# Stage a of an rfft on float16 parts of x, with x read once for its maximum and once more for the products, and its loads on GpSimd's queue

## The chip, the cores and the metric

The kernel runs on one core of one Trainium2 chip. The metric is the device time of one execution in microseconds (us). Before the change the median of 3 runs is 2065.36 us (2063.82 to 2065.78). A separate execution was taken with the hardware profiler; all rows of the trace come from that one.

## The reference

x has 8 batches of 3072 rows by 256 columns, float32. The sequence axis goes through a real FFT, the 256 columns through a complex product with bias and a soft threshold, then the inverse FFT; what comes out is put, row by row, through three products of 256 by 768, their maximum, and a product of 768 by 256.

```
X = np.fft.rfft(x, axis=1)
Yr = Xr @ w_r - Xi @ w_i + b_r
Yi = Xr @ w_i + Xi @ w_r + b_i
Yr = np.sign(Yr) * np.maximum(np.abs(Yr) - lam, 0.0)   # Yi likewise, lam = 0.01
y = np.fft.irfft(Yr + 1j * Yi, n=3072, axis=1)
h = np.maximum(np.maximum(y @ w1, y @ w2), y @ w3)
out = (h @ w_out).astype(np.float32)
```

## The kernel before, in words

**Stages.** The transform of 3072 points is cut into 96 by 32. Stage a is the transform over 96 points (product with the 96x96 table fr): a batch of x is seen as (n1 = 96, n2 = 32, 256 columns) and worked on in eight *quads* of four n2 each; q = 8 * batch + i numbers the quads. A quad has two halves of 96x512. Its result goes through DRAM (a_d). Stage b is the transform over 32 points (tiles px, 12 steps k in a batch), stage w the complex product and the soft threshold (tiles py), stage q a first part of the inverse (tiles pz), whose result goes through DRAM again (z_d). `inverse` (tiles pi) then makes the input yh, yl of the dense part. `up` makes three tiles pu of 128x384 with 18 matmuls of 384 columns, the maximum of which (tiles c and h, lines 757 to 760 on ScalarE and VectorE) is split into float16 halves hh; `down` (tiles pd) multiplies these by w_out with 9 matmuls of 256 columns.

**Products in parts.** A product in high precision is three matmuls (`mm3`, lines 132 to 134): high by high, high by low, low by high. The parts are made by two instructions for a tile: ScalarE writes the high part (line 121 in `split`, 126 in `split_scaled`), VectorE the rest (122, 127). `split_scaled` multiplies by a power of two first. Nearly all parts are float16. Those of stage a are float32r (`x_tile(...).bitcast(F32R)`, fh and fl), and these are made only from quad NATIVE = 16 on, so for batches 2 to 7; batches 0 and 1 take x as it is in one float32 matmul for a half (line 434).

**Stage a in detail.** `load_x` (398) loads a quad, 384 KB, into a tile xq of a pool with two buffers (six quads of batch 0 go to other tiles, xr), by SyncE's queue. `split_x` (410) takes the largest |x| of each half on VectorE (416, tile mxx) and makes the parts. `stage_a` (427) has the matmuls into a PSUM tile pa, ScalarE's copy to SBUF (437) and the store to a_d, by ScalarE's queue (by GpSimd's for batch 0). Behind the last quad of a batch, lines 441 to 452 make the scales of the batch from its largest |x| by a chain of small instructions: s0x scales what `split_a` (459) splits for stage b, s0v the later parts.

**Order.** The dense part goes in *slots*: one slot is one f of `up` and `down`, six for a quad of z, so SLOTS = 48 for a batch, 384 in all. The stages of the next batches are laid between the slots by a list `events` (lines 682 to 702): each entry has a position in slots, a function and its number, and the entries up to a slot's position are run behind that slot. For a quad of batches 2 to 7 the load is at p - 3, `split_x` at p, `stage_a` at p + 1, with p = (b - 2) * 48 + 6i + 2; so a batch's quads are spread over the 48 slots two batches ahead of it, and its stage b to q over the next 48. Batch 1's quads stand at p = i. A scheduler then fixes the order on each engine, and each engine runs its list in order.

## Time and profile before

| | before |
|---|---|
| median of 3 runs | 2065.36 us |
| the profiled execution | 2070.11 us |
| its span, first to last instruction | 2068.3 us |
| granted TensorE clock, mean | 0.995 |
| moved by DMA | 165.13 MB, 80 GB/s in the mean |
| loads of x (xq and xr) | 64 of 384 KB, all by SyncE's queue |

How to read it. PE is TensorE's matmuls, PEld its weight loads, DVE VectorE, ACT ScalarE, POOL GpSimd, SP SyncE; an engine's name with a q behind it is its DMA queue. A group of instructions is told by its line, engine and operation, the tile written, an arrow and the tiles read, the shape, how many there are, then their busy time, the mean of one in ns, and the idle time ahead of them with what ended it. Matmuls overlap, so the mean of one is longer than the distance between two; a timeline, which has each instruction's start, gives the distance. L132 to L134 are the three matmuls of `mm3`, wherever it is called.

### The profile page before, as it was taken

Reading aid. Unit: us, or ns where it says so; the run is one execution under the profiler, and the core shown is the slowest. Engines: PE = TensorE matmul, PEld = TensorE weight load, DVE = VectorE, ACT = ScalarE, POOL = GpSimd, SP = SyncE. Lnnn points to the kernel's source line nnn. Section 1 sums busy time; section 2 is a strip of 40 time slices with the busy share of each in tenths; the row PEclk is TensorE's granted clock in tenths of the full one; section 3 lists DMA queues with packets and bytes.
Section 4 is the critical chain, followed back from the end, with each engine's and each line's share of the span. In section 5 each row is a group of like instructions: output and inputs, shape, how many; then the busy total and the mean of one; then the engine's idle time right before and its main releaser. Section 6 shows DMA issues by size and latency. Waiting matters only on the chain.

```text
span 2068.3 us, 38435 instructions
## 1 busy us (share of the span) xinstructions
PE 2040.7 (99%) x15500; PEld 1431.4 (69%) x15500; DVE 1547.9 (75%) x3043; ACT 1035.0 (50%) x2051; POOL 27.6 (1%) x79
## 2 busy tenths in 40 slices
PE   8999999999999999999999999999999999999998
PEld 5756766677776767767776777767777777776666
DVE  3987897678867888678886788767887578865543
ACT  4755554455545555455554455445554445433333
POOL 1000000000000000000000000000000000000000
PEclk9999999999999999999999999999999999999999
DMA  9454221322213222223213222132221212111100
GB/s 311 141 155 123 90 70 52 107 68 89 75 52 100 79 84 62 65 83 92 85 60 97 62 78 87 47 100 72 86 74 44 77 52 67 42 47 32 34 30 23
DMA packets 106694, 165.13 MB, mean 80 GB/s; under 512 B 9795, under 2 KB 85059, under 8 KB 106419
## 3 DMA queue, kind: packets, MB, share of 16 engines
q1 hardware_dynamic: 45347, 86.69, 14.4%
q10 hardware_dynamic: 60032, 72.37, 10.6%
q0 software_dynamic: 1136, 3.61, 0.5%
q8 instruction: 121, 1.98, 0.4%
q14 instruction: 58, 0.48, 0.1%
HBM read 87.14 MB, written 75.50 MB: 79 GB/s over the span
## 4 chain that ended last, share of the span: by engine, by line
PE 82%; DVE 10%; DMA 3%; ACT 2%; issue 2%; ACTq 0%; SPq 0%; DVEq 0%
PE pu L134 16%; PE pu L132 16%; PE pu L133 16%; PE pd L134 5%; PE pd L132 5%; PE pd L133 5%; PE py L132 2%; PE py L133 2%; PE py L134 2%; DMA xq<-in_x_dram 2%; DVE u L620 1%; PE pi L132 1%; PE pa L434 1%; DVE h L760 1%; PE pa L133 1%
## 5 line engine op out<-in xcount | busy, mean ns | idle before, releaser
L132 PE MATMUL pu<-yh,wuh 128*128 128x384 f16 x2304 | 752.6, 327 | 2.2 <-DVE c L758 1.1
L133 PE MATMUL pu<-yl,wuh 128*128 128x384 f16 x2304 | 751.7, 326 | 0.0
L134 PE MATMUL pu<-yh,wul 128*128 128x384 f16 x2304 | 751.7, 326 | 0.0
L126 ACT ACTIVATE hh<-h 128x384 f16<-128x384 f32 x384 | 200.4, 522 | 512.3 <-DVE h L760 509.8
L134 PEld LDWEIGHTS <-wul 128*128 128x128 f16 x2304 | 225.5, 98 | 148.9 <-issue 1.1
L132 PEld LDWEIGHTS <-wuh 128*128 128x128 f16 x2304 | 225.9, 98 | 143.4 <-issue 14.7
L133 PEld LDWEIGHTS <-wuh 128*128 128x128 f16 x2304 | 225.9, 98 | 135.1 <-issue 5.8
L758 DVE TENSOR_TENSOR c<-pu,c 128x384 f32<-128x384 f32 x384 | 212.5, 554 | 136.8 <-PE pu L134 76.3
L127 DVE SCALAR_TENSOR_TENSOR hh<-h,hh 128x384 f16<-128x384 f32 x384 | 213.6, 556 | 135.3 <-ACT hh L126 132.0
L134 PE MATMUL pd<-woh,hh 128*128 128x256 f16 x1152 | 313.6, 273 | 0.9 <-DVE hh L127 0.8
L132 PE MATMUL pd<-woh,hh 128*128 128x256 f16 x1152 | 313.9, 273 | 0.4 <-ACT hh L126 0.3
L133 PE MATMUL pd<-wol,hh 128*128 128x256 f16 x1152 | 313.8, 273 | 0.0
L760 DVE TENSOR_TENSOR h<-pu,c 128x384 f32<-128x384 f32 x384 | 212.7, 554 | 45.6 <-PE pu L134 33.8
L757 ACT ACTIVATE c<-pu 128x384 f32<-128x384 f32 x384 | 186.0, 484 | 102.7 <-PE pu L134 98.6
L620 DVE SCALAR_TENSOR_TENSOR u<-py,s1x,cs 64x256 f32<-64x256 f32 x308 | 148.5, 482 | 40.9 <-ACT cs L631 30.9
L132 PE MATMUL py<-wch,tt 128*128 128x256 f16 x504 | 137.4, 273 | 0.4 <-DVE yl L127 0.4
L134 PE MATMUL py<-wch,tt 128*128 128x256 f16 x504 | 137.4, 273 | 0.0
L133 PE MATMUL py<-wcl,tt 128*128 128x256 f16 x504 | 137.4, 273 | 0.0
L132 PEld LDWEIGHTS <-hh 128*128 128x128 f16 x1152 | 112.7, 98 | 34.3 <-ACT hh L126 1.0
L133 PEld LDWEIGHTS <-hh 128*128 128x128 f16 x1152 | 112.7, 98 | 33.4
L783 ACT ACTIVATE o<-pd,s1u 128x256 f32<-128x256 f32 x192 | 83.6, 469 | 90.9 <-PE pd L134 53.3
L134 PEld LDWEIGHTS <-hh 128*128 128x128 f16 x1152 | 112.7, 98 | 15.3 <-DVE hh L127 2.0
(205 smaller groups left out, 2889.6 us busy)
## 6 DMA issues: line engine op xcount, KB each, us to landing
aj<-a_d SPq DMA_DIRECT2D x96, 256.0 KB, 2.8
z_d<-zs ACTq DMA_DIRECT2D x96, 256.0 KB, 2.1
out_dram<-o ACTq DMA_DIRECT2D x192, 128.0 KB, 2.1
zq<-z_d SPq DMA_DIRECT2D x63, 384.0 KB, 3.5
xq<-in_x_dram SPq DMA_DIRECT2D x58, 384.0 KB, 4.0
a_d<-aq ACTq DMA_DIRECT2D x56, 384.0 KB, 3.0
rw<-in_moe_w_dram SPq DMA_DIRECT2D x6, 768.0 KB, 9.4
xr<-in_x_dram SPq DMA_DIRECT2D x6, 384.0 KB, 11.4
```

The source lines that it names most:

```text
L126: nc.scalar.activation(out=hi, in_=src, func=AF.Copy, scale=scale)
L127: nc.vector.scalar_tensor_tensor(out=lo, in0=src, scalar=scale, in1=h, op0=ALU.mult, op1=ALU.subtract)
L132: nc.tensor.matmul(o, lh, rh, start=start, stop=False, **kw)
L133: nc.tensor.matmul(o, lh, rl, start=False, stop=False, **kw)
L134: st["mm"] = nc.tensor.matmul(o, ll, rh, start=False, stop=stop, **kw)
L434: nc.tensor.matmul(pa[0:96], fr, xp, start=True, stop=True)
L620: nc.vector.scalar_tensor_tensor(out=u[64 * c:64 * c + 64, j], in0=pk[r], scalar=inv[r], in1=c1[r], op0=ALU.mult, op1=ALU.add,)
L757: nc.scalar.activation(out=c1, in_=pu[0], func=AF.Copy)
L758: nc.vector.tensor_tensor(out=c1, in0=pu[1], in1=c1, op=ALU.max)
L760: nc.vector.tensor_tensor(out=h32, in0=pu[2], in1=c1, op=ALU.max)
L783: nc.scalar.activation(out=o, in_=pd[t], func=AF.Copy, scale=st[b, "su"][1])
```

## The change

- fh and fl become float16 (times 2^10), and the two parts of x for batches 2 to 7 become float16, made by `split_scaled` with a new scale s2x of the batch. The parts of a half lie side by side in one tile: xh for half 0 and xl for half 1. ScalarE's copy behind the matmuls takes a factor 2^-17.
- s2x needs the largest |x| of the whole batch ahead of the parts. So the maximum leaves `split_x` for a function of its own, `largest_x`, and x of batches 2 to 7 is loaded twice: for the maximum at position m - 3 (maximum at m), and for the products at p - 3. m = (b - 3) * 48 + 6i + 5 for batches 3 to 7, that is one batch ahead of the products, and 8 + 2i for batch 2, whose products move from 6i + 2 to 24.5 + 2.9i.
- The chain that makes the scales is now the function `scale_x`, behind the last maximum of a batch (for batch 1 behind its last quad, as before).
- a comes out of stage a already scaled, so `split_a` of batches 2 to 7 uses `split` in place of `split_scaled`.
- x is loaded by GpSimd's queue but for batch 0.

```diff
-    fh = const.tile([N1, 96], F32R, name="fh")
-    fl = const.tile([N1, 96], F32R, name="fl")
+    fh = const.tile([N1, 96], F16, name="fh")
+    fl = const.tile([N1, 96], F16, name="fl")
...
-            nc.sync.dma_start(out=xq.rearrange("p (n d) -> p n d", n=NQ), in_=xv)
+            eng = nc.sync if q < NCH else nc.gpsimd
+            eng.dma_start(out=xq.rearrange("p (n d) -> p n d", n=NQ), in_=xv)
...
+    def largest_x(q):
+        b, q4 = divmod(q, NCH)
+        for i, xp in enumerate(st["x", q]):
+            nc.vector.tensor_reduce(
+                out=batch(b, "x")[0:N1, 2 * q4 + i:2 * q4 + i + 1], in_=xp, axis=AX.X,
+                op=ALU.max, apply_absolute_value=True,
+            )
+        if b > 1 and q4 == NCH - 1:
+            scale_x(b)
+    def scale_x(b):
+        low, add = st["lim", "x"]
+        e = exponent_of(st.pop((b, "x"))[0:N1], "x", 23, 0xFF, low)
+        st[b, "sx"] = power("s0x", e, -1.0, 261.0), power("s1x", e, 1.0, add)
+        if b > 1:
+            st[b, "sx2"] = power("s2x", e, -1.0, 268.0)
...
             if q >= NATIVE:
-                xh, xl = (x_tile(n).bitcast(F32R)[0:N1] for n in ("xh", "xl"))
-                split(xh, xl, xp)
+                t = x_tile(("xh", "xl")[i]).bitcast(F16)[0:N1]
+                xh, xl = t[:, 0:2 * D], t[:, 2 * D:4 * D]
+                split_scaled(xh, xl, xp, st[b, "sx2"][0:N1])
...
-            nc.scalar.activation(out=aq[:, i * 512:i * 512 + 512], in_=pa[0:96], func=AF.Copy)
+            nc.scalar.activation(
+                out=aq[:, i * 512:i * 512 + 512], in_=pa[0:96], func=AF.Copy,
+                scale=1.0 if q < NATIVE else A_SCALE,
+            )
...
-        split_scaled(ah, al, aj, st[k // NJP, "sx"][0])
+        if k // NJP > 1:
+            split(ah, al, aj)
+        else:
+            split_scaled(ah, al, aj, st[k // NJP, "sx"][0])
...
-        p = i if b == 1 else (b - 2) * SLOTS + NF * i + 2
+        p = i if b == 1 else 24.5 + 2.9 * i if b == 2 else (b - 2) * SLOTS + NF * i + 2
+        if b > 1:
+            m = 8 + 2 * i if b == 2 else (b - 3) * SLOTS + NF * i + 5
+            at(m - 3, load_x, q)
+            at(m, largest_x, q)
         at(p - 3, load_x, q)
...
-    split(fh, fl, fr)
+    split_scaled(fh, fl, fr, F_SCALE)
```

How the order of the instructions moves is shown at three places. In the rows a number behind a tile's name tells its buffer use apart; lines are those of each kernel's own file (before 406 and after 408 are the loads of x, 416 and 415 the maximum, 758 and 784 the first maximum of three products, 760 and 786 the second).

The first place is the border of two batches near slot 97, on VectorE. Before, the two loads xq_8031 and xq_8453 are read for their maxima in the slots behind the border:

```order
L760 TENSOR_TENSOR h32_7685<-pu_7675,c1_7682 128x384
L127 SCALAR_TENSOR_TENSOR al_8083<-aj_7879,s0x_7568,ah_8082 128x512
L127 SCALAR_TENSOR_TENSOR hh_7687<-h32_7685,hh_7687 128x384
L416 TENSOR_REDUCE mxx_7830<-xq_8031 96x1 x2
L758 TENSOR_TENSOR c1_7722<-pu_7708,c1_7722 128x384
L760 TENSOR_TENSOR h32_7725<-pu_7715,c1_7722 128x384
L127 SCALAR_TENSOR_TENSOR hh_7727<-h32_7725,hh_7727 128x384
L416 TENSOR_REDUCE mxx_7830<-xq_8453 96x1 x2
```

After, at the same place, xq_7738 and xq_8100 hold quads for the products, xq_8283 and xq_8730 quads for their maxima; the pool still has two buffers:

```order
L128 SCALAR_TENSOR_TENSOR xl_7905<-xq_7738,s2x_7758,xl_7905 96x512
L784 TENSOR_TENSOR c1_7843<-pu_7829,c1_7843 128x384
L786 TENSOR_TENSOR h32_7846<-pu_7836,c1_7843 128x384
L128 SCALAR_TENSOR_TENSOR xh_8277<-xq_8100,s2x_7758,xh_8277 96x512
L128 SCALAR_TENSOR_TENSOR xl_8280<-xq_8100,s2x_7758,xl_8280 96x512
L128 SCALAR_TENSOR_TENSOR hh_7848<-h32_7846,hh_7848 128x384
L415 TENSOR_REDUCE mxx_8102<-xq_8283 96x1 x2
L784 TENSOR_TENSOR c1_7885<-pu_7871,c1_7885 128x384
L786 TENSOR_TENSOR h32_7888<-pu_7878,c1_7885 128x384
L128 SCALAR_TENSOR_TENSOR hh_7890<-h32_7888,hh_7890 128x384
L415 TENSOR_REDUCE mxx_8102<-xq_8730 96x1
L784 TENSOR_TENSOR c1_7931<-pu_7917,c1_7931 128x384
```

The load of xq_8283 goes into the buffer that xq_7738 leaves when the row xl_7905 and ScalarE's half of that split have read it; the load of xq_8730 goes into the same buffer when the maxima of xq_8283 have read that. So there is one slot between the row xl_7905 and the maxima of xq_8283, and one between these and the maxima of xq_8730. Both kinds of maxima stand ahead of a c1, the first step of the maximum over the three products. Slots 49, 145 and 193 have the same sequence; slot 241 has not.

The second place is the queue of the loads at the same border. Before, on SyncE's queue, the loads of x stand between the loads aj of stage b and the loads zq of the inverse:

```order
L406 DMA xq_7699<-in_x_dram 96x1024
L713 DMA zq_7460<-z_d_5224 96x1024
L713 DMA zq_7790<-z_d_5224 96x1024
L457 DMA aj_7748<-a_d_4606 128x2x256
L457 DMA aj_7879<-a_d_4606 128x2x256
L406 DMA xq_8031<-in_x_dram 96x1024
L713 DMA zq_8147<-z_d_5224 96x1024
L457 DMA aj_8080<-a_d_4606 128x2x256
L457 DMA aj_8266<-a_d_4606 128x2x256
L406 DMA xq_8453<-in_x_dram 96x1024
```

After, they stand on GpSimd's queue, where the border has GpSimd's own work on the last step of stage w (L583 to L593):

```order
L408 DMA xq_7738<-in_x_dram 96x1024
L408 DMA xq_7908<-in_x_dram 96x1024
L583 TENSOR_SCALAR tt_7010<-tt_7010 128x4x64
L591 COPY ts_7015<-tt_7010 128x256
L593 MEMSET ts_7015 128x2 x2
L583 TENSOR_SCALAR tt_7010<-tt_7010 128x4x64
L591 COPY ts_7019<-tt_7010 128x256
L593 MEMSET ts_7019 128x2 x2
L408 DMA xq_8100<-in_x_dram 96x1024
L408 DMA xq_8283<-in_x_dram 96x1024
```

On SyncE's queue the rows aj and zq now follow one another; the loads of x wait on GpSimd for a buffer of their own pool, and behind the last step of stage w.

The third place is batch 0's slots 5 to 9 on VectorE, where no product of batch 2 stands any more. Before:

```order
L758 TENSOR_TENSOR c1_1256<-pu_1242,c1_1256 128x384
L416 TENSOR_REDUCE mxx_835<-xq_1055 96x1
L760 TENSOR_TENSOR h32_1259<-pu_1249,c1_1256 128x384
L416 TENSOR_REDUCE mxx_835<-xq_1055 96x1
L127 SCALAR_TENSOR_TENSOR yl_1286<-pi_1287,yh_1285 128x384
L127 SCALAR_TENSOR_TENSOR hh_1261<-h32_1259,hh_1261 128x384
L127 SCALAR_TENSOR_TENSOR yl_1286<-pi_1302,yh_1285 128x384
L758 TENSOR_TENSOR c1_1338<-pu_1324,c1_1338 128x384
L416 TENSOR_REDUCE mxx_835<-xq_1153 96x1
L760 TENSOR_TENSOR h32_1341<-pu_1331,c1_1338 128x384
L416 TENSOR_REDUCE mxx_835<-xq_1153 96x1
```

After:

```order
L784 TENSOR_TENSOR c1_1369<-pu_1355,c1_1369 128x384
L786 TENSOR_TENSOR h32_1372<-pu_1362,c1_1369 128x384
L415 TENSOR_REDUCE mxx_1345<-xq_1153 96x1 x2
L128 SCALAR_TENSOR_TENSOR hh_1374<-h32_1372,hh_1374 128x384
L784 TENSOR_TENSOR c1_1426<-pu_1412,c1_1426 128x384
L415 TENSOR_REDUCE mxx_835<-xq_1205 96x1 x2
L786 TENSOR_TENSOR h32_1429<-pu_1419,c1_1426 128x384
L415 TENSOR_REDUCE mxx_835<-xq_1259 96x1 x2
L128 SCALAR_TENSOR_TENSOR hh_1431<-h32_1429,hh_1431 128x384
L208 TENSOR_REDUCE col_1505<-mxx_835 96x1
```

There xq_1153 is the first quad of batch 2 and the others are batch 1's. The load of xq_1205 goes into the buffer that the maxima of xq_1153 leave, three rows ahead of its own maxima, which now stand between a c1 and its h32.

More of the change, by code (lines that the diff above doesn't have):

```diff
@@ L22 @@
 T_SCALE, Y_SCALE, H_SCALE, Q_SCALE = 2.0**-15, 2.0**-14, 2.0**-22, 2.0**12
+A_SCALE, F_SCALE = 2.0**-17, 2.0**10
 def dft_tables():
@@ L405, in load_x @@
                 xq = fft.tile([N1, NQ * D], F32, name="xq", bufs=2)
-            nc.sync.dma_start(out=xq.rearrange("p (n d) -> p n d", n=NQ), in_=xv)
+            eng = nc.sync if q < NCH else nc.gpsimd
+            eng.dma_start(out=xq.rearrange("p (n d) -> p n d", n=NQ), in_=xv)
             pairs = [xq[:, i * 2 * D:(i + 1) * 2 * D] for i in range(2)]
         st["x", q] = pairs
+    def largest_x(q):
[13 more added lines that the diff above has]
+            st[b, "sx2"] = power("s2x", e, -1.0, 268.0)
+        m = small("mv", bufs=2)
+        nc.vector.tensor_scalar(
+            out=m, in0=e, scalar1=add, scalar2=st["eb"], op0=ALU.add, op1=ALU.max
+        )
+        nc.vector.tensor_scalar(out=m, in0=m, scalar1=230.0, scalar2=None, op0=ALU.min)
+        st[b, "sv"] = power("s0v", m, -1.0, 231.0), power("s1v", m, 1.0, 11.0)
     def split_x(q):
         b, q4 = divmod(q, NCH)
-        pairs = st.pop(("x", q))
+        if b == 1:
+            largest_x(q)
         parts = []
-        for i, xp in enumerate(pairs):
-            if b:
-                nc.vector.tensor_reduce(
-                    out=batch(b, "x")[0:N1, 2 * q4 + i:2 * q4 + i + 1], in_=xp, axis=AX.X,
-                    op=ALU.max, apply_absolute_value=True,
-                )
+        for i, xp in enumerate(st.pop(("x", q))):
             if q >= NATIVE:
-                xh, xl = (x_tile(n).bitcast(F32R)[0:N1] for n in ("xh", "xl"))
-                split(xh, xl, xp)
+                t = x_tile(("xh", "xl")[i]).bitcast(F16)[0:N1]
+                xh, xl = t[:, 0:2 * D], t[:, 2 * D:4 * D]
+                split_scaled(xh, xl, xp, st[b, "sx2"][0:N1])
                 xp = xh, xl
@@ L436, in stage_a @@
                 mm3(pa[0:96], fh, fl, *xp)
-            nc.scalar.activation(out=aq[:, i * 512:i * 512 + 512], in_=pa[0:96], func=AF.Copy)
+            nc.scalar.activation(
+                out=aq[:, i * 512:i * 512 + 512], in_=pa[0:96], func=AF.Copy,
+                scale=1.0 if q < NATIVE else A_SCALE,
+            )
         (nc.scalar if b else nc.gpsimd).dma_start(
@@ L440, in stage_a @@
         )
-        if b and q4 == NCH - 1:
-            low, add = st["lim", "x"]
-            e = exponent_of(st.pop((b, "x"))[0:N1], "x", 23, 0xFF, low)
-            st[b, "sx"] = power("s0x", e, -1.0, 261.0), power("s1x", e, 1.0, add)
-            m = small("mv", bufs=2)
-            nc.vector.tensor_scalar(
-                out=m, in0=e, scalar1=add, scalar2=st["eb"], op0=ALU.add, op1=ALU.max
-            )
-            nc.vector.tensor_scalar(out=m, in0=m, scalar1=230.0, scalar2=None, op0=ALU.min)
-            st[b, "sv"] = power("s0v", m, -1.0, 231.0), power("s1v", m, 1.0, 11.0)
+        if b == 1 and q4 == NCH - 1:
+            scale_x(b)
     def load_a(k):
```

## The prediction

> **What bounds the kernel now.** I read the page first, its busy times and the chain that ended last, then the groups of instructions by shape, and last the timelines of the places where the change acts. The page's lines, with the load of x among the DMA issues (count, KB, microseconds from issue to landing):
>
> ```profile
> span 2068.3 us, 38435 instructions
> PE 2040.7 (99%) x15500; PEld 1431.4 (69%) x15500; DVE 1547.9 (75%) x3043; ACT 1035.0 (50%) x2051; POOL 27.6 (1%) x79
> PE 82%; DVE 10%; DMA 3%; ACT 2%; issue 2%; ACTq 0%; SPq 0%; DVEq 0%
> xq<-in_x_dram SPq DMA_DIRECT2D x58, 384.0 KB, 4.0
> ```
>
> TensorE is busy 99% of the span and 82% of the chain: the kernel is a long row of matmuls. Time goes down where matmuls become shorter or one of TensorE's few waits goes, and up where VectorE, at 75%, or a load makes it wait. VectorE's share is a mean over stages. First the part where the dense part runs alone with the later batches (637 to 886 us), then two pieces of batch 0's slots; columns are the length, the busy time of PE, PEld, DVE, ACT and POOL, the granted clock, the DMA share and GB/s:
>
> ```profile
> 637.00:886.00 249.00, 247.98 (x1945) 175.62 (x1944) 196.25 (x380) 129.08 (x257) 2.92 (x8) 1.00 0.25 77
> 143.80:208.50 64.70, 63.01 (x465) 41.71 (x464) 46.80 (x99) 33.17 (x67) 0.00 (x0) 1.00 0.41 123
> 242.00:289.00 47.00, 44.63 (x365) 31.34 (x363) 40.84 (x77) 24.87 (x50) 0.00 (x0) 0.96 0.32 97
> ```
>
> In the first TensorE is full and VectorE has a fifth of its time free. In the third (slots 23 to 29) VectorE is at 40.84 of 47.00 and TensorE waits 2.4 us: there VectorE sets the pace with it.
>
> **Shorter products.** The change halves no count: 48 quads keep six matmuls of 512 columns each. What each costs now is read from starts on TensorE's timeline, since matmuls overlap. A quad among products of the dense part, and one that is followed by stage b:
>
> ```profile
> 676.94 0.27 PE L132 MATMUL pd<-woh,hh 128*128 128x256 f16 x1
> 677.05 0.27 PE L133 MATMUL pd<-wol,hh 128*128 128x256 f16 x1
> ...
> 677.84 0.47 PE L132 MATMUL pa<-xh,fh 96*96 96x512 f32 x1
> ...
> 679.32 0.34 PE L132 MATMUL pu<-yh,wuh 128*128 128x384 f16 x1
> 679.49 0.33 PE L133 MATMUL pu<-yl,wuh 128*128 128x384 f16 x1
> ```
>
> ```profile
> 959.04 0.58 PE L132 MATMUL pa<-xh,fh 96*96 96x512 f32 x1
> ...
> 960.82 0.22 PE L132 MATMUL px<-mb_all,ah 128*128 128x128 f16 x1
> ```
>
> Six matmuls take 679.32 - 677.84 = 1.48 us; next to px 1.78, as the step between float32 and float16 kinds shows more. Float16 products of the same 512 columns stand in stage q:
>
> ```profile
> 1254.92 0.38 PE L132 MATMUL pz<-vp,qh 128*128 128x512 f16 x1
> ...
> 1255.57 0.33 PE L132 MATMUL pu<-yh,wuh 128*128 128x384 f16 x1
> ```
>
> Three take 0.65, one 0.216 us, six 1.30. So a quad gives 1.48 - 1.30 = 0.18 us, 48 quads **8.6 us**, and six of them (one in a batch, ahead of px) 0.3 us more each, **1.8 us**. All of this lies on TensorE's path where TensorE is full, as it is in most of the span. Bounds: 0 if a 96-row float16 product went no faster than the float32 one, and nothing beyond 10.4.
>
> **The splits.** What the parts cost on VectorE and ScalarE by the groups (count | busy, mean ns | idle before):
>
> ```profile
> L416 DVE TENSOR_REDUCE mxx<-xq 96x1 f32<-96x512 f32 x112 | 74.2, 675 | 17.7 <-DMA xq<-in_x_dram 17.5
> L122 DVE TENSOR_TENSOR xl<-xq,xh 96x512 fp32r<-96x512 f32 x96 | 65.2, 684 | 18.3 <-ACT xh L121 18.3
> L127 DVE SCALAR_TENSOR_TENSOR al<-aj,s0x,ah 128x512 f16<-128x512 f32 x84 | 62.7, 747 | 5.1 <-ACT ah L126 3.4
> L126 ACT ACTIVATE ah<-aj,s0x 128x512 f16<-128x512 f32 x84 | 60.0, 716 | 7.2 <-DMA aj<-a_d 4.8 <-PE px L133 2.3
> L121 ACT ACTIVATE xh<-xq 96x512 fp32r<-96x512 f32 x96 | 58.6, 620 | 3.8 <-DMA xq<-in_x_dram 3.8
> ```
>
> The parts of x turn from the plain into the scaled kind: VectorE 747 - 684 = 63 ns, 96 times, +6.0 us, ScalarE 716 - 620 = 96 ns, 96 times, +9.2 us. Those of a turn the other way for batches 2 to 7 (72 tiles): -4.5 and -6.9 us. Net +1.5 us on VectorE, +2.3 on ScalarE, both beside TensorE (196 and 129 us of 249 above); if the cover were gone, at most these 1.5 us. The number of maxima stays 112. I count them at nothing after batch 0.
>
> **The border of two batches.** Here a load of x is late now. The chain from the last quad of batch 2 on (600 to 650 us; start, length), then VectorE's wait, then TensorE:
>
> ```profile
> 624.62 4.52 DMA a_d<-aq
> 629.16 0.38 SPq L457
> 629.59 0.46 SPq L457
> 630.10 5.42 DMA xq<-in_x_dram
> ```
>
> ```profile
> 635.54 1.28 DVE L416 TENSOR_REDUCE mxx<-xq 96x1 f32<-96x512 f32 x2 [0.63 <-DMA xq<-in_x_dram]
> ```
>
> ```profile
> 640.24 0.27 PE L134 MATMUL pd<-woh,hh 128*128 128x256 f16 x1
> 640.93 0.32 PE L132 MATMUL pu<-yh,wuh 128*128 128x384 f16 x1 [0.42 <-ACT c L757]
> ...
> 1139.01 0.33 PE L134 MATMUL pu<-yh,wul 128*128 128x384 f16 x1
> 1140.20 0.32 PE L132 MATMUL pu<-yh,wuh 128*128 128x384 f16 x1 [0.86 <-DVE c L758]
> ```
>
> On SyncE's queue the load of x stands behind loads aj that wait for the store of a. Its landing is 5.4 us after that, the maxima hold up VectorE, and TensorE loses 0.69 - 0.11 = 0.58 us here and 1.19 - 0.16 = 1.03 at the border after next. The two other borders show some 0.1 and 0.6 in the same way. On GpSimd's queue nothing waits for a store: **-2.3 us**.
>
> In its place comes a wait of the pool's two buffers. By the order, from xl_7905 to the c1 behind the first maximum of xq_8730 there are two round trips of a load (L each, from a buffer's last reader to the landing) and three maxima (distance 0.6), in the time of two slots. A slot is 18 matmuls pu at 0.163 us and 9 pd at 0.109 (679.32 to 679.49, 676.94 to 677.05): 3.91 us, two 7.8. VectorE may be late by some 2.1 us before TensorE stands, by my estimate: pu has three buffers, so the next matmul that needs the one c1 reads is three groups of 0.98 us away, less c1's own 0.6 and its hand-over. So a border costs 2L + 1.8 - 9.9: 0 at L = 4.05, 0.9 at 4.5, 1.9 at 5, 3.9 at 6. What is queued behind the waiting maximum is c1, h32 and hh, and TensorE waits for these. Behind the waiting load on GpSimd are the next loads only; its own work L583 to L593 stands ahead, behind two loads whose buffers came free some ten slots before.
>
> L is not in the trace for GpSimd. Rows near it: SyncE's load at 4.0 us in the median, and what GpSimd needs to issue and land transfers of the same size (in the start, when all DMA engines are full):
>
> ```profile
> L438 POOL DMA_DIRECT2D a_d<-ga_sb x3 | 1.5, 505 | 2.5 <-ACT ga_sb L437 2.4
> ```
>
> ```profile
> a_d<-ga_sb POOLq DMA_DIRECT2D x3, 384.0 KB, 8.6
> ...
> a_d<-wuh POOLq DMA_DIRECT2D x2, 384.0 KB, 6.6
> ```
>
> ```profile
> 20.00:30.00 10.00, 7.49 (x34) 3.13 (x32) 1.95 (x4) 0.95 (x2) 0.80 (x2) 1.00 0.81 315
> ```
>
> At the borders the DMA share is near 0.25, not 0.81, so I take the quiet load's 4.0 and GpSimd's 0.5 of issue: L = 4.5, at four borders 4 x 0.85 = **+3.4 us**; ends 0 (L = 4) and +15.6 (L = 6). The Trainium skill's page "DMA: Bandwidth & Descriptors", section "Anatomy of one DMA — SWDGE (gpsimd) path", fits 2.0 us plus bytes over 436e3, an estimate of 2.9 us for 384 KB, by which this term would be 0 and the sum 3.4 us lower. The rows at hand are all longer than that, the quiet median of 4.0 us among them, so I stay with 4.5.
>
> **Batch 0's slots.** VectorE gets most of batch 3's maxima more (batch 2's are there anyway): by the order 12 more in slots 0 to 48, 12 x 0.675 = 8.1 us. They come early: slots 4 to 16 have 18 maxima more and 6 parts xl less, 18 x 0.6 - 6 x 0.6 = +7 on 46.80 of 64.70. TensorE loses batch 2's first quads there, 2 x 1.5 us, and gets them back in slots 27 to 47. In slots 23 to 29 the order has some 5 us more for VectorE (four parts xh, one xl, al, vp, zl more), which is 46 on the 47.00 that these took. So each piece just holds it. TensorE's waits in this part that may go:
>
> ```profile
> 274.03 0.47 PE L132 MATMUL pa<-xh,fh 96*96 96x512 f32 x1 [2.37 <-ACT zs L675]
> ...
> 275.42 0.52 PE L133 MATMUL pu<-yl,wuh 128*128 128x384 f16 x1
> 275.74 0.52 PE L134 MATMUL pu<-yh,wul 128*128 128x384 f16 x1
> ```
>
> A gap of 2.4 us, then pu at distances of 0.32 instead of 0.163 until 277.9: 4 us for one wait. Against it stands the load of xq_1205, a round trip within a slot: 4.5 us less the slack of 2.1 and some 1.5 us of rows between, +1 to +2. I take **0**, from -6 (the gaps go) to +5 (VectorE's extra 5 us show).
>
> **The start and the second read.** Two loads of batch 1 now leave in the start, among GpSimd's stores: 0.79 MB, at 315 GB/s (row 20:30) 2.5 us of full DMA engines. The stage b that follows waits for such a store:
>
> ```profile
> 21.50 6.21 DMA a_d<-wuh
> ```
>
> I take half, **+1.4 us** (0 to 2.7). The other second reads, 48 x 384 KB = 18.9 MB, go on 77 GB/s of traffic at a share of 0.25: hidden. GpSimd's 104 issues of 0.505 us are 53 us on an engine with 27.6 busy: hidden, and without that cover it is the round trip above.
>
> **Sum.** -8.6 - 1.8 - 2.3 + 3.4 + 0 + 1.4 = -7.9 us. On the profiled execution (2070.11, of it 2068.3 in the span) that gives 2062.2; that execution is 4.75 above the median, and I take the difference over to it: 2065.4 - 7.9 = **2057.4 us**.
>
> **Rivals.** *Slower: the round trip.* If GpSimd's loads take 6 us (6.6 to 8.6 in the start speaks for it; SyncE's 4.0 in quiet stages, and 5.4 even beside aj, against), the borders cost 15.6 and xq_1205 and the like 3 more than I took: -7.9 + 12.2 + 3 = +7.3, **2072.7**. It decides from where 8 (L - 4.5) passes 7.9 + 4.1, without the rest: L = 6.0; with it from 5.6 on. Chance 0.2.
>
> *No change: VectorE in batch 0.* L = 5 (+4.0 more) and half of the 5 us in slots 23 to 29 shows: -1.4, **2064**. For it: 46 of 47; against: there are gaps of 2.4 us that fall to other work. Chance 0.21.
>
> *Batch 0 gains.* The gap at 274 and its slow matmuls go without a new one: -4 more, 2053; 0.14, inside the forecast's side.
>
> *The lock.* VectorE's fast passes could stop GpSimd from writing a load's descriptors. The one such group with an uncommonly short time for its size is
>
> ```profile
> L577 DVE TENSOR_SCALAR t<-u 128x512 f32<-128x512 f32 x84 | 35.3, 420 | 0.9
> ```
>
> 35.3 us, 1.7% of the span. If each of eight border trips met one, +8 x 0.42 = 3.4 us: 2060.8. The Trainium skill says in "SBUF — State Buffer", section "SBUF: two separate sides", that a VectorE operation in a two-port mode and a GpSimd operation exclude each other, whichever began first, which is the rule that speaks against this change. No row of before shows it. Chance 0.05, still faster.
>
> **How the numbers follow.** Forecast 0.40, batch 0 gains 0.14, the lock 0.05: faster by over 0.2% (4.1 us, about what a measurement of this kernel can tell) 0.58 in round numbers; same 0.21; slower 0.21. The forecast's own range is 2050 to 2061 (L 4 to 5, start 0 to 2.7, some of batch 0). To hold 8 in 10 it reaches up to the slower rival, 2073, and down to 2047 (batch 0 at -6, L = 4).
>
> **What would show it.** Right: groups pa by float16 with quads of 1.30 us start to start; mxx waiting at slots 49, 97, 145, 193 for xq, under 1 us of TensorE's gap at each; xq landing at 4 to 4.5 us on POOLq; no wait of SyncE ahead of xq. Wrong: landings of 6 us; TensorE gaps of 3 us at borders; a VectorE share over 95% with TensorE gaps in 230 to 290 us; px starting over 2 us later than 30.9 us; or quads still at 1.48.

## The result, and the profile after

| | before | after |
|---|---|---|
| median | 2065.57 us (4 runs) | 2090.33 us (4 runs, 2089.76 to 2091.20) |
| ratio | | 1.0115, 95% interval 1.0100 to 1.0129 |
| the profiled execution | 2070.11 us | 2089.76 us |
| its span | 2068.3 us | 2088.0 us |

The kernel became 24.8 us slower; 8 us faster was forecast. The page of after: its span, the busy times, the chain that ended last, and the load of x among the DMA issues.

```profile
span 2088.0 us, 38552 instructions
...
PE 2041.7 (98%) x15500; PEld 1423.0 (68%) x15500; DVE 1549.6 (74%) x3061; ACT 1036.2 (50%) x2051; POOL 79.7 (4%) x183
...
PE 62%; DVE 12%; issue 12%; ACT 4%; DMA 3%; ACTq 1%; POOL 0%; DVEq 0%; POOLq 0%; SPq 0%
...
xq<-in_x_dram POOLq DMA_DIRECT2D x104, 384.0 KB, 4.0
```

Only GpSimd has much more to do than before, 79.7 against 27.6 us, and it is idle for 96% of the span: VectorE 1549.6 against 1547.9 us, ScalarE 1036.2 against 1035.0. A load of x on GpSimd's queue lands in 4.0 us, as it did on SyncE's. What changed is the chain: TensorE has 62% of it, before 82%, and 12% is "issue" and 12% VectorE. TensorE now waits more, and for the other engines.

Where it waits is read from a mark that every slot has: the start of h, the second step of the maximum, of which there are 384. Two of them on VectorE's timeline, h of slot 48 (the first of batch 1) and of slot 288 (batch 6, when the last quads of stage a are done), of before and of after:

```profile
388.21 0.56 DVE L760 TENSOR_TENSOR h<-pu,c 128x384 f32<-128x384 f32 x1
...
1632.52 0.56 DVE L760 TENSOR_TENSOR h<-pu,c 128x384 f32<-128x384 f32 x1 [0.35 <-PE pu L134]
```

```profile
397.31 0.55 DVE L786 TENSOR_TENSOR h<-pu,c 128x384 f32<-128x384 f32 x1
...
1652.03 0.56 DVE L786 TENSOR_TENSOR h<-pu,c 128x384 f32<-128x384 f32 x1 [0.35 <-PE pu L135]
```

After is 9.1 us late at slot 48 and 19.5 at slot 288; at slot 0 it is 5.1 late (121.82 against 116.73), and behind slot 288 it loses 0.2 more. So 5.1 us are lost in the start, 4.0 in batch 0's slots, and 10.4 in slots 48 to 288, where the prediction had most of its gain. This lag behind before is the measure of all experiments below. Each lag compares one profiled execution with one. That of before took 2070.11 us, 4.5 above its median, so the lag at the end, 19.7 us, is less than the 24.8 of the medians, and a difference of one to three us between two lags shows little.

**The start.** After's GpSimd queue, then TensorE's first product of stage b in before and in after:

```profile
12.48 0.52 POOL L408 DMA_DIRECT2D xq<-in_x_dram  x1
...
20.80 0.51 POOL L408 DMA_DIRECT2D xq<-in_x_dram  x1 [0.50 <-PE pa L460]
21.86 0.51 POOL L467 DMA_DIRECT2D a_d<-wuh  x1 [0.56 <-DMA a_d<-aq]
```

```profile
30.89 0.79 PE L481 MATMUL px<-mb_all,aj 128*128 128x128 f32 x5 [3.40 <-DMA aj<-a_d]
```

```profile
33.01 2.05 PE L503 MATMUL px<-mb_all,aj 128*128 128x128 f32 x8 [5.51 <-DMA aj<-a_d]
```

The two loads stand among the stores of a, and px starts at 33.01 instead of 30.89.

**A quad.** TensorE's timeline around one quad of after:

```profile
1361.74 0.27 PE L135 MATMUL py<-wch,ts 128*128 128x256 f16 x1
1361.85 0.38 PE L133 MATMUL pa<-xh,fh 96*96 96x512 f16 x1
...
1363.14 0.33 PE L133 MATMUL pu<-yh,wuh 128*128 128x384 f16 x1
```

The matmul that stands ahead of the prediction's quoted quad, which began at 677.84, on before's timeline:

```profile
677.82 0.27 PE L134 MATMUL pd<-woh,hh 128*128 128x256 f16 x1
```

Six float16 matmuls take 1363.14 - 1361.85 = 1.29 us, as forecast. But the first float32r matmul is recorded 0.02 us behind the matmul ahead of it, which needs 0.11; the float16 one 0.11 behind its own. From the last foreign matmul to the next one a quad took 679.32 - 677.82 = 1.50 us and takes 1363.14 - 1361.74 = 1.40. The gain is 0.10 us, not 0.18. A quad ahead of px (behind pz) takes 1.80 us from the last foreign matmul to px in both kernels and gains nothing.

**A border of batches.** After's VectorE in slots 51 and 52, TensorE two slots on, and GpSimd's issue:

```profile
411.07 0.56 DVE L128 SCALAR_TENSOR_TENSOR hh<-h,hh 128x384 f16<-128x384 f32 x1 [0.59 <-ACT hh L127]
413.52 1.27 DVE L415 TENSOR_REDUCE mxx<-xq 96x1 f32<-96x512 f32 x2 [1.90 <-DMA xq<-in_x_dram]
414.71 0.74 DVE L128 SCALAR_TENSOR_TENSOR xh<-xq,s2x,xh 96x512 f16<-96x512 f32 x1
415.37 0.74 DVE L128 SCALAR_TENSOR_TENSOR xl<-xq,s2x,xl 96x512 f16<-96x512 f32 x1
```

```profile
420.29 0.27 PE L135 MATMUL pd<-woh,hh 128*128 128x256 f16 x1
421.59 0.32 PE L133 MATMUL pu<-yh,wuh 128*128 128x384 f16 x1 [1.03 <-ACT c L783]
```

```profile
409.64 0.51 POOL L408 DMA_DIRECT2D xq<-in_x_dram  x1 [3.68 <-DVE mxx L415]
```

VectorE waits 1.90 us for the maximum's load, which GpSimd (third fence) issued at 409.64, when the maxima ahead of it had read the buffer. That is the round trip of the prediction, at 413.52 - 409.64 = 3.9 us. The gap in TensorE comes 8 us later. From 413.52 until that gap VectorE waits only once more, 0.59 us ahead of hh at 417.83, so what it lost it hardly makes up; that this lateness is what TensorE's gap is made of is read from the order, not tested.

**The second half of an inverse.** TensorE at slot 71, before and after:

```profile
503.52 0.33 PE L133 MATMUL pu<-yl,wuh 128*128 128x384 f16 x1
504.08 0.22 PE L132 MATMUL pi<-ga_sb,zh 96*128 96x96 f16 x1 [0.23 <-ACT c L757]
```

```profile
514.46 0.32 PE L133 MATMUL pu<-yh,wuh 128*128 128x384 f16 x1
515.75 0.22 PE L133 MATMUL pi<-ga_sb,zh 96*128 96x96 f16 x1 [0.96 <-DVE u L642]
```

The second half of pi stands behind four matmuls pu instead of eight, 0.65 us further ahead, and waits for VectorE's u, which frees its PSUM tile. Nothing in the diff touches this line. The scheduler placed it anew.

### The profile page after: what moved, and what is told of

Read it like the earlier page. It is cut to its first block, busy times and chain, and to the rows that moved or that the text cites. A ratio compares the mean times of both kernels' runs of the same rounds, so it can differ in the third digit from the quotient of the medians.

```text
span 2088.0 us, 38552 instructions
## 1 busy us (share of the span) xinstructions
PE 2041.7 (98%) x15500; PEld 1423.0 (68%) x15500; DVE 1549.6 (74%) x3061; ACT 1036.2 (50%) x2051; POOL 79.7 (4%) x183
## 4 chain that ended last, share of the span: by engine, by line
PE 62%; DVE 12%; issue 12%; ACT 4%; DMA 3%; ACTq 1%; POOL 0%; DVEq 0%; POOLq 0%; SPq 0%
PE pu L135 12%; PE pu L134 12%; PE pu L133 12%; PE pd L135 4%; PE pd L133 4%; PE pd L134 4%; DVE u L642 2%; DMA xq<-in_x_dram 2%; DVE h L786 2%; PE py L135 2%; PE py L133 2%; PE py L134 2%; DVE c L784 2%; DVE hh L128 1%; PE pi L133 1%
## 5 line engine op out<-in xcount | busy, mean ns | idle before, releaser
L134 PEld LDWEIGHTS <-wuh 128*128 128x128 f16 x2304 | 225.7, 98 | 146.7 <-issue 13.3
```

Source lines behind the costliest of these rows:

```text
L134: nc.tensor.matmul(o, lh, rl, start=False, stop=False, **kw)
```

## The experiments

The theories: A, the two buffers of x; B, GpSimd's queue; C, the second read as such; D, the order that the scheduler gives to everything else. A table behind the experiments has the lags that the argument uses.

**Undoing one part.**

```diff
# e1_sync_queue: the changed kernel, all loads of x on SyncE
-            eng = nc.sync if q < NCH else nc.gpsimd
-            eng.dma_start(
+            nc.sync.dma_start(
# e2_own_buffers: the changed kernel, loads for the maxima into raw_tile
-            at(m - 3, load_x, q)
+            at(m - 3, load_m, q)
# e3_f16_fixed_scale: the kernel before with float16 parts, one read
-                split(xh, xl, xp)
+                split_scaled(xh, xl, xp, X_SCALE)
# e4_one_read: the changed kernel, maxima taken in split_x, parts by X_SCALE
-        if b == 1:
+        if b:
             largest_x(q)
```

> The changed kernel with every load of x on SyncE's queue again. Theory A (the buffers: the loads for the maxima and for the products share two buffers, so a load waits for the last reader and VectorE then waits a round trip of some 4 us, whichever queue issues it): no gain, 2088 to 2100 us, since on SyncE a load that waits for its buffer also holds up the loads aj and zq behind it. Theory B (the queue: GpSimd's loads are late): the 24.8 us go, 2057 to 2070. Theory C (the second read as such, VectorE's work and its order in batch 0 and at the borders): 2085 to 2092, no difference.

2117.35 us, ratio 1.0239 (1.0224 to 1.0255). Theory B falls in its plain form: without GpSimd's queue the second read is worse by 27 us. The time lies above all three expected ranges; TensorE's pi alone waits 23.8 us for VectorE's u, at 12 places.

> The changed kernel with the loads for the maxima of batches 2 to 7 in buffers of their own (the eight tiles of 6 KB that only the start uses), so that no such load waits for a reader of a quad for the products, and the other way round. Theory A: the waits of VectorE at slots 50 to 53, 98, 146, 194 go (some 2.5 to 3 us at each of the three later borders, more in batch 0): 2072 to 2080. Theory B: 2088 to 2092, as the queue is the same. Theory C: 2085 to 2092.

2091.34 us, ratio 1.0114 (1.0097 to 1.0131): no gain in the whole. But the lag grows by 3.2 us from slot 48 to 288, not 10.4; it grows by 10.1 ahead of slot 48, not 4.0. That would be theory A at the borders, some 7 us of it, but the edit did one thing more: the maxima, no longer held back by the two buffers, are done earlier, 86 of them in slots 0 to 48, where after has 44, and none behind slot 96. So the borders have no maximum left that could wait.

> The kernel before with float16 parts in stage a at a fixed scale of 2^15 (enough for this x), without a second read, all loads and positions as before; stage a's copy takes 2^-25. This is the first term alone. By the terms of the prediction (8.6 + 1.8 us): 2055. By the starts in the trace of after (a quad from the matmul ahead of it 1.41 instead of 1.50 us, so some 0.08 a quad, 3 to 4 us in all): 2061 to 2063. Each theory of the loss (A, B, C) expects no loss here.

2091.83 us, ratio 1.0117 (1.0099 to 1.0134). None of A, B and C had this: float16 parts alone, with nothing read twice and no queue changed, cost as much as the whole change. In five batches TensorE has a wait for VectorE's u which before has not. Its timeline at the first of them, and the row of stretches around it (length, busy times, granted clock, DMA share, GB/s):

```profile
503.86 0.22 PE L133 MATMUL pi<-ga_sb,zh 96*128 96x96 f16 x1 [2.03 <-DVE u L625]
...
504.60 0.52 PE L135 MATMUL pu<-yh,wul 128*128 128x384 f16 x1
504.91 0.53 PE L133 MATMUL pu<-yh,wuh 128*128 128x384 f16 x1
...
507.47 0.37 PE L135 MATMUL pu<-yh,wul 128*128 128x384 f16 x1
507.67 0.33 PE L133 MATMUL pu<-yh,wuh 128*128 128x384 f16 x1
```

```profile
495.00:520.00 25.00, 22.97 (x178) 16.03 (x177) 19.67 (x37) 13.96 (x29) 0.00 (x0) 0.93 0.28 85
```

The wait is 2.03 us (2.4, 2.3, 2.4 and 3.6 at 756.76, 1011.62, 1264.69 and 1522.70), and behind it nine pu take 2.87 us instead of 9 x 0.163 = 1.47. So each of the first four places costs some 3.7 us, 15 of the 25 by which e3's profiled execution lags more at slot 288 than at slot 48. VectorE is late there because it waited for a load of x behind two loads aj on SyncE's queue:

```profile
500.86 0.68 DVE L417 TENSOR_REDUCE mxx<-xq 96x1 f32<-96x512 f32 x1 [1.20 <-DMA xq<-in_x_dram]
...
502.82 2.00 DVE L625 SCALAR_TENSOR_TENSOR u<-py,s1x,cs 64x256 f32<-64x256 f32 x4
```

> The changed kernel without the second read: the maxima are taken where the products' parts are made, as before, the parts at a fixed scale of 2^15; loads from batch 1 on by GpSimd's queue, batch 2's products at their new positions. Theories A and C: the loss goes but for the start, 2060 to 2068. Theory B: 2080 or more, as every load of x still comes by GpSimd's queue.

2085.85 us, ratio 1.0087 (1.0072 to 1.0102). Without the second read 18 us of the loss stay, where A and C expected 2060 to 2068; B's 2080 or more is met, but e13 below speaks against B.

**Adding one part to the kernel before.**

```diff
# e5_batch1_sync: the changed kernel, batch 1's loads on SyncE
-            eng = nc.sync if q < NCH else nc.gpsimd
+            eng = nc.sync if q < NATIVE else nc.gpsimd
# e6_own_late: e5 and own buffers for the maxima of batches 4 to 7
+        load_x(q, q >= 4 * NCH)
# e7_before_gpsimd (the kernel before), e8_f16_gpsimd (e3)
-            nc.sync.dma_start(out=xq
+            eng = nc.sync if q < NATIVE else nc.gpsimd
+            eng.dma_start(out=xq
```

> The changed kernel with batch 1's loads of x on SyncE's queue as before; batches 2 to 7 stay on GpSimd's. What the start costs by GpSimd's queue. Slot 0 comes 5.1 us later after than before, and 0.4 later with all loads on SyncE. If the two loads among the start's stores are the cause: 4 to 5 us less than after, 2085 to 2087. If what is lost there is given back by slot 3 (there after is 1.7 us ahead of before): 2089 to 2091.

2086.01 us, ratio 1.0086 (1.0067 to 1.0105), 4 to 6 us less than after: the start.

> The same as the run before it in this call, and the loads for the maxima of batches 4 to 7 (slots 53 on) in buffers of their own. Own buffers for all maxima took the borders' delay away (from slot 48 to slot 288 the lag behind before grew by 3 us, in after by 10) but cost 8 us more ahead of slot 48. If the borders' waits are the two buffers (theory A, for the borders alone): 6 to 8 us less than the run before it, 2078 to 2081. If not: the same within 2 us.

2085.91 us, ratio 1.0087 (1.0069 to 1.0106). The lag from slot 48 to 288 grows by 3.0 instead of 9.1, as in e2, and in slots 0 to 48 by 9 more than in e5. No gain in sum again, which A did not expect. The maxima moved as in e2: 92 in slots 0 to 48 against 46 in e5.

> The kernel before with one thing changed: x of batches 2 to 7 by GpSimd's queue. Theory B (GpSimd's loads are late): 2075 to 2090. By the prediction's third term, the waits behind aj at the borders go: 2063. Theory D (the order on TensorE and VectorE that the scheduler gives to before is a good one by chance, and every edit, whatever it does, changes it: the second half of an inverse, pi, then stands 0.65 us further ahead and waits for the instruction u of VectorE): 2070 to 2085, though no instruction got longer.

2081.99 us, ratio 1.0064 (1.0044 to 1.0084): one word of the change, and over half of its loss. Its loads land in 3.9 us:

```profile
xq<-in_x_dram POOLq DMA_DIRECT2D x48, 384.0 KB, 3.9
```

What did change is seen at slot 60. VectorE's timeline of the kernel before, then of this one:

```profile
444.98 0.56 DVE L758 TENSOR_TENSOR c<-pu,c 128x384 f32<-128x384 f32 x1
445.45 0.68 DVE L643 TENSOR_TENSOR u<-u,bias 128x512 f32<-128x512 f32 x1
446.05 0.55 DVE L760 TENSOR_TENSOR h<-pu,c 128x384 f32<-128x384 f32 x1
```

```profile
446.38 0.67 DVE L417 TENSOR_REDUCE mxx<-xq 96x1 f32<-96x512 f32 x1
446.98 1.97 DVE L621 SCALAR_TENSOR_TENSOR u<-py,s1x,cs 64x256 f32<-64x256 f32 x4
448.98 0.69 DVE L644 TENSOR_TENSOR u<-u,bias 128x512 f32<-128x512 f32 x1
449.70 0.56 DVE L759 TENSOR_TENSOR c<-pu,c 128x384 f32<-128x384 f32 x1
450.18 0.42 DVE L578 TENSOR_SCALAR t<-u 128x512 f32<-128x512 f32 x1
450.51 0.55 DVE L761 TENSOR_TENSOR h<-pu,c 128x384 f32<-128x384 f32 x1
```

u with the bias now stands ahead of c and a maximum ahead of the four u, so h, hh, ScalarE's zs and the next c are late, and TensorE's timeline has behind px:

```profile
453.86 0.22 PE L134 MATMUL px<-mb_all,al 128*128 128x128 f16 x1
454.57 0.32 PE L132 MATMUL pu<-yh,wuh 128*128 128x384 f16 x1 [0.49 <-ACT c L758]
```

a gap of 0.71 - 0.06 = 0.65 us, once in each batch, and others of its kind. Why the order moved is read in the code and not tested by a run of its own: load_x queues a load behind the last load of stage b by `tc.issue_after(st["ld"].ins)`, which orders only what is on the same engine as that load. On GpSimd's queue the line orders nothing, and the scheduler is free to take x to be there earlier and to move what reads it. e6 agrees: the first of its loads into own buffers, which `events` puts at slot 50, is issued at 97.67 us, ahead of slot 0 (115.70).

> The kernel before with float16 parts at a fixed scale, one read, batch 2's positions as before, and x of batches 2 to 7 by GpSimd's queue. With the parts alone on SyncE's queue 2091.8, a load late at slot 71 of each batch because it stands behind loads aj that wait for a buffer. If that is all: 2062 to 2066. Theory D: 2072 to 2085. Theory C (the second read): below before.

2084.54 us, ratio 1.0079 (1.0056 to 1.0102). The order from slot 96 to 144 is that of e7 on all three engines, yet the quads' 0.1 us each does not show: 3.1 us slower than e7 by the ratios.

**Changing the order alone.**

```diff
# e9_before_pinned: the kernel before; e10: e7; e11: e8; e12: e5 (and largest_x)
+    def in_slot(a):
+        with tc.issue_after(st["hh"].ins):
+            a[0](a[1])
...
-        at(p, split_x, q)
+        at(p, in_slot if b > 1 else split_x, q if b == 1 else (split_x, q))
```

> The kernel before with an edit of order alone: what VectorE does for x of batches 2 to 7 (the maxima and the low parts) is queued behind the part hh of the slot it belongs to, never between a c1 and its hh. Same instructions, sizes and queues. Theory D (the time hangs on how VectorE's order falls, and before's order is a good one that every edit gives up): off by over 5 us, most likely slower, 2070 to 2085. If order hardly matters: 2064 to 2069.

2072.43 us, ratio 1.0027 (1.0018 to 1.0037). An edit that adds no work and changes no queue costs 5.5 us. It gains 7.8 us up to slot 48 and loses 9.4 behind.

> The same with x of batches 2 to 7 by GpSimd's queue. From slot 49 on the order on TensorE, VectorE and ScalarE is instruction for instruction that of the run before it, so the two differ by the queue alone. Theory B (the queue is slow): 8 to 13 us slower than the run before it. Theory D (GpSimd's queue cost 13 us on the kernel before only because it let the scheduler order VectorE anew): within 3 us of it, or faster, since no load stands behind aj any more.

2074.79 us, ratio 1.0034 (1.0024 to 1.0045). By the queue alone, with one order from slot 49 on: 1.4 us more than e9 by the ratios, whose intervals overlap.

> The same with the float16 parts at a fixed scale. Against the run before it: the quads are shorter by 0.08 to 0.1 us each, 3 to 5 us in all, and VectorE's part is 60 ns longer. Theory D, with the order held: 2 to 5 us faster than the run before it. If the float16 parts cost time by themselves: slower.

2082.66 us, ratio 1.0076 (1.0056 to 1.0097). Slower by 8.7 us than e10, where 2 to 5 faster was expected. This pin leaves ScalarE and a few rows of VectorE free, and these fell otherwise.

> The changed kernel with batch 1's loads on SyncE and the same pin on its maxima and low parts. Without the pin 2086.0. Theory D: 2072 to 2080, if the maxima and parts ahead of hh were the loss. Theory C (the second read costs by itself, through VectorE's work and the two buffers): 2084 to 2092.

2099.26 us, ratio 1.0154 (1.0130 to 1.0179). A miss: the pin makes the changed kernel worse by 13 us. Low parts behind hh are not the cure.

**Holding the whole order.** The next three carry a table of the order that the kernel before has on TensorE, VectorE and ScalarE, and chain every instruction to its predecessor there (order alone, no waits).

```diff
# e13: e7; e14: e8; e15: e3
+    for name, text in ORDERS.items():
+        rows = np.cumsum(np.frombuffer(zlib.decompress(base64.b85decode(text)), dtype="<i4"))
+        mine = [i for i in traced if i.engine == getattr(mybir.EngineType, name)]
+        for r, s in zip(rows, rows[1:]):
+            tc.add_manual_dep(mine[s], mine[r].name, NO_SYNC, reason="order")
```

> The kernel before with x of batches 2 to 7 by GpSimd's queue, and the order of every instruction on TensorE, VectorE and ScalarE held to that of the kernel before (without that 2082.0). Theory D (the queue cost 13 us because the scheduler ordered VectorE and ScalarE anew): 2062 to 2069. Theory B (the queue itself): 2075 to 2082.

2068.57 us, ratio 1.0001 (0.9992 to 1.0009). The queue's 13 us are gone, and so is theory B for the kernel before. The chain that ended last, of e7 and of e13:

```profile
PE 45%; issue 27%; DVE 17%; ACT 6%; DMA 4%; POOL 1%; ACTq 1%; SPq 0%; DVEq 0%; POOLq 0%
```

```profile
PE 79%; DVE 11%; DMA 3%; ACT 3%; issue 3%; ACTq 0%; SPq 0%; DVEq 0%; POOLq 0%
```

With the old order the chain is close to before's, 82% TensorE there.

> The same with the float16 parts at a fixed scale, order held to that of before (without that 2084.5). If the shorter quads count where the order leaves them the path: 3 to 5 us faster than the run before it, 2059 to 2065. If VectorE takes all of it back at the next wait: the same as the run before it. If float16 parts cost time: slower.

2070.23 us, ratio 1.0010 (1.0001 to 1.0018). Of e8's 16 us (queue and float16 parts) 2 are left, and nothing is gained: the case in which VectorE takes the gain back at the next wait. In the profiled executions it is 2.3 us ahead of e13, of which 1.7 in slots 48 to 288; but e13's was the slowest of its eleven, and by the medians e14 is 1.7 us behind.

> The float16 parts at a fixed scale with x on SyncE's queue, order held to that of before on TensorE, VectorE and ScalarE (without that 2091.8). Theory D: 2060 to 2066. If the late load at slot 71 was due to SyncE's queue and not to the order: 2080 or more.

2074.25 us, ratio 1.0029 (1.0015 to 1.0043), against 1.0117 without the held order. Between the two cases: most of e3's loss was order.

**Holding the rest.** The changed kernel has instructions that before has not, so only the others can be held: all but the loads, maxima, parts, products and scales of stage a for batches 2 to 7, which fall where the scheduler puts them.

```diff
# e16: the changed kernel; e17: e5; e18: e6
-            at(m, largest_x, q)
+            at(m, marked(largest_x), q)
...
+    traced = [i for i in nc.cur_bb.bb.instructions if i.name not in apart]
```

> The changed kernel, with everything on TensorE, VectorE and ScalarE that is not the loads, maxima, parts, products and scales of batches 2 to 7's stage a held to the order it has in the kernel before; those are left to fall where the scheduler puts them. Theory D (the order of the rest): the 13 us that the queue cost go, 2074 to 2080, and what is left is the start (about 6), the second read and the parts. If the loss sits in the second read and its place: 2086 to 2092.

2092.93 us, ratio 1.0119 (1.0100 to 1.0138).

> The same with batch 1's loads on SyncE's queue. Theory D: 4 to 6 us less than the run before it, 2068 to 2075, near the kernel before. Else: 2082 to 2086, as without the held order (2086.0).

2089.57 us, ratio 1.0094 (1.0068 to 1.0121).

> The same with the loads for the maxima of batches 4 to 7 in buffers of their own. If VectorE's waits for the two buffers at the borders (about 2 us each at four borders) lie on the path once the order of the rest is held: 4 to 8 us less than the run before it. If they are taken up by slack: the same within 2 us.

2089.83 us, ratio 1.0104 (1.0077 to 1.0130). In the whole D misses here: the changed kernel does not come back when the rest has its old order. The lags say where (us behind the kernel before, in the profiled executions):

| kernel | slot 0 | slot 48 | slot 288 | 0 to 48 | 48 to 288 | maxima in slots 0 to 48 |
|---|---|---|---|---|---|---|
| after | 5.1 | 9.1 | 19.5 | 4.0 | 10.4 | 44 |
| e1 SyncE's queue | 0.4 | 1.3 | 45.6 | 1.0 | 44.2 | 44 |
| e2 own buffers | 6.9 | 16.9 | 20.1 | 10.1 | 3.2 | 86 |
| e5 batch 1 on SyncE | 1.8 | 6.2 | 15.3 | 4.4 | 9.1 | 46 |
| e6 e5, own buffers | -1.0 | 12.6 | 15.6 | 13.6 | 3.0 | 92 |
| e7 queue alone | 2.9 | 2.4 | 12.2 | -0.6 | 9.8 | 34 |
| e8 queue and float16 | 3.4 | 3.5 | 13.3 | 0.1 | 9.8 | 36 |
| e13 e7, order held | 2.7 | 1.6 | 0.5 | -1.2 | -1.1 | 32 |
| e14 e8, order held | 2.0 | 0.4 | -2.4 | -1.6 | -2.8 | 32 |
| e16 after, rest held | 7.0 | 19.6 | 22.7 | 12.5 | 3.1 | 46 |
| e17 e5, rest held | 2.5 | 17.2 | 19.6 | 14.8 | 2.4 | 46 |
| e18 e6, rest held | 1.4 | 25.5 | 19.8 | 24.0 | -5.7 | 92 |

Own buffers (e2, e6, e18) take 6 to 8 us off the growth in slots 48 to 288 and put 6 to 9 us on that in slots 0 to 48. The last column says why this does not price the two buffers: some 45 maxima change sides. What reads mxx or writes it on VectorE in slots 0 to 48 of e5 and of e6 (length, busy time, granted clock, DMA share, GB/s):

```profile
118.50:394.40 275.90, 30.91 (x49) 0.99 0.39 113
```

```profile
115.70:400.80 285.10, 60.48 (x95) 0.98 0.52 149
```

That is 30 us of VectorE's work moved into the slots where VectorE is shortest of time, and away from the borders. The move and the wait for a buffer are not told apart by these runs, and e18's gain of 5.7 us behind slot 48 is not that of the kernel that the prediction described.

The held order moves no maxima and takes 7.3 us off after's 10.4 (e16) and 6.7 off e5's 9.1 (e17), though in e17 VectorE still waits 1.8 to 2.0 us for a load of x at the borders of slots 97, 145 and 193. One quad falls ahead of slot 48 instead of behind it, so some 1.4 us of this is a shift. In slots 0 to 48 the held order does harm. On e17's timelines of VectorE and of TensorE:

```profile
157.14 0.68 DVE L460 TENSOR_REDUCE mxx<-xq 96x1 f32<-96x512 f32 x1 [4.15 <-DMA xq<-in_x_dram]
```

```profile
158.34 0.48 PE L178 MATMUL pu<-yh,wuh 128*128 128x384 f16 x1 [3.54 <-DVE h L841]
```

VectorE waits for a load into the shared two buffers, the row h of slot 6 stands behind that maximum, and TensorE waits for h. From slot 4 to slot 8 the lag goes from -0.7 to 7.2. e5 has the same wait of VectorE (3.44 us at 155.85), but with h ahead of it, and its lag is -2.8 at both slots. e16 has it too, 4.80 us at 162.00. So the round trip within a slot that the prediction saw in batch 0 costs nothing in one order, and in another it stands behind the longest wait in a loss of 8 us.

## Why the prediction was wrong, step by step

**The step that failed first is the one that was not taken.** The prediction priced the order only where the edit puts instructions, and put the order of all the rest at nothing, without a reason. "On GpSimd's queue nothing waits for a store: -2.3 us" is true of the queue, and the queue costs nothing (e13: 1.0001). But that word alone moved the scheduler's choice on all three engines, and in a kernel without any other change 13 us were lost (e7). The three places at which the orders were compared ahead of the run do not have TensorE's pi among them, and no term was given to it. On the changed kernel itself the held order takes back 7 us behind slot 48 (e16) and not the whole, so the 13 us are shown on the kernel before and only in part on this one. In the ladder of runs, each ratio times 2067: the queue 13.2, float16 parts 3.1 more, the second read with its new scale and positions 1.4 more, batch 1's loads in the start 6.0 more, 23.8 in all. The steps are not independent, since each brings a new order; each term is uncertain by some 4 us.

**"VectorE may be late by some 2.1 us before TensorE stands."** L was taken at 4.5; the loads land in 4.0. The price 2L + 1.8 - 9.9 would then have been 0. The waits came where they were foretold: 1.9 us at 413.52, and at slots 97, 145 and 193 up to 1.9, 1.8 and 2.0. What they cost by themselves no run isolates. From slot 48 to 240, the four batches that begin with such a border, the lag grows by 8.8 us in after, and by 2.0 in e17, which has the same waits and the old order of the rest; the prediction's net for the borders was 3.4 - 2.3 = 1.1. So the mechanism was right, and its price depends on the order around it: the slack of 2.1 us is slack for one lateness, and in after VectorE has only 0.59 us of idle time between the wait and TensorE's gap 8 us later.

**The quads: 0.18 us each.** The product takes 1.29 us as forecast. The other end was wrong: the start of the first float32r matmul is recorded early, beside the one ahead of it. The extra 0.3 us ahead of px was no gain at all, since these quads take 1.80 us from pz to px before and after. 0.10 us for the other 43 is 4.3 us, not 8.6 and 1.8; and of these, with order and queue held, the profiled executions show 2.3 (e14 against e13) and the medians none. TensorE reaches the next wait for VectorE earlier and waits longer there. The groups of e13 and of e14 between 390 and 1632 us (count | busy, mean ns | idle time ahead):

```profile
L185 PE MATMUL pi<-ga_sb,zh 96*128 96x96 f16 x320 | 45.3, 206 | 1.2 <-DVE u L674 0.2
```

```profile
L186 PE MATMUL pi<-ga_sb,zh 96*128 96x96 f16 x320 | 45.3, 206 | 3.6 <-DVE u L679 2.7
```

The wait for u grew by 2.5 us in these two executions. By them, that part of the prediction ("all of this lies on TensorE's path where TensorE is full") is wrong in the stretches with stage b to w, where TensorE is 99% busy and still follows VectorE.

**The splits at nothing.** The groups of after:

```profile
L123 DVE TENSOR_TENSOR al<-aj,ah 128x512 f16<-128x512 f32 x72 | 49.5, 687 | 10.4 <-ACT ah L122 10.2
...
L128 DVE SCALAR_TENSOR_TENSOR xl<-xq,s2x,xl 96x512 f16<-96x512 f32 x48 | 35.7, 744 | 5.3 <-ACT xl L127 4.8
L128 DVE SCALAR_TENSOR_TENSOR xh<-xq,s2x,xh 96x512 f16<-96x512 f32 x48 | 35.7, 743 | 13.4 <-ACT xh L127 12.9
```

The durations were right, 744 and 743 ns where 747 was taken, al 687 where 684. That the 1.5 us in the sum are free was not tested by itself: the kernels with a fixed scale (e3, e8, e11, e14) do not have this term, since their low parts take 681 to 685 ns (e3, e14).

**The start: +1.4.** px is 2.1 us late, which is within the bounds and just over the 2 us that the prediction named as a sign of being wrong; but slot 0 is 5.1 us late, and the start costs 4 to 6 us (e5). The last store of a lands at 30.05 us instead of 27.72. How 2.1 us at px become 5.1 at slot 0 was not followed.

**Batch 0: 0, from -6 to +5.** 4.0, inside. That it came out inside is in part luck: with the same count of maxima and the rest in its old order 12.5 us are lost there (e16), and a wait of the kind of xq_1205's, priced at +1 to +2, is 4.80 us long.

**The rivals.** The slower one, a round trip of 6 us, gave 2072.7 with the wrong cause: L was 4.0. The lock did not show. The issues of x on GpSimd, from the loads' own view (minimum, median and longest in ns):

```profile
L408 POOL DMA_DIRECT2D xq<-in_x_dram x104: 505/505/559, 12.5 to 1518.0; - x104
```

None of 104 took more than 559 ns, and the median is that of before's stores, 505. That a VectorE operation in a two-port mode and a GpSimd operation lock each other out, as the Trainium skill says in "SBUF — State Buffer", section "SBUF: two separate sides", cost nothing that these rows show. The Trainium skill's page "DMA: Bandwidth & Descriptors", section "Anatomy of one DMA — SWDGE (gpsimd) path", would have had the load at an estimated 2.9 us; the trace has 4.0, and the measurement decides. By the prediction's own formula the borders would have been free at either. The rival "VectorE in batch 0" had the right place for 4 us of the 24.8.

**What stays open.** What the wait for the two buffers costs with the maxima in their places, why after and e5 lose 4 us in slots 0 to 48, and how much of after's whole loss is order, since no kernel with the second read came back to the time of before. The pinned kernels e9 and e10 are 6 to 8 us ahead of before at slot 48, and the held order is best behind it; a kernel that joins the two was not tried. No run beats the kernel before.

## What to carry to other kernels

An edit's price has a term that the diff does not show: the order that the scheduler gives to all the rest, which here cost 13 us for one changed queue on the kernel before and was got back there by holding the old order; so compare the orders of instructions that the edit does not touch, and measure a change once with the order held. A constraint that orders work on one engine is lost without a word when the work goes to another. A remedy can move work besides what it is meant to do, as the own buffers did with the maxima; so count where the work is done before its effect is put down to the remedy. Shorter matmuls are worth their gain only up to TensorE's next wait, and their pitch is measured from the last matmul of another kind, not from the first of their own.

## What the runs showed of the hardware

A wait of TensorE can cost more than its length. In e3's rows above, 2.03 us without matmuls are followed by pu at distances of 0.32 us from 504.60 until 507.47, 3.6 us behind the first pi, and then 0.163 again; the granted clock of that stretch is 0.93. The Trainium skill, "TensorE: Matmul & The Clock Gate", section "What's actually happening", puts the half rate behind an idle window of about 3.4 us and the return after about 3.4 us of work: the return agrees, but here a gap of 2.0 us was enough. The length of the gap alone does not decide it: in after a gap of 1.61 us ahead of pi at 245.25 is followed by pu at 0.32 us, and one of 2.23 us ahead of pi at 322.04 by pu at 0.163.

A load of 384 KB took as long from GpSimd's queue (4.0 us in after, 3.9 in e7) as from SyncE's (4.0).
